# Last second products of the first pass placed between the next pass's first products, on four PSUM banks, with memory given back in two lots

## The chip, the cores and the metric

One Trainium2 chip, one core. The metric is device time in microseconds (us): how long one execution of the whole program takes. A measurement of this kernel is the median of several executions.

## What is computed

Three layers follow one another: a retention layer (attention with decay, 4 sequences of 576 tokens, 8 heads of 64), a mixture of experts in which each token goes to its best expert, and a second mixture in which every token goes through all eight experts and is weighted by a normalised gate P. The change lies in the third:

```python
def _moe2_ref(x, w_gate, w1, w2):            # x [2304,512], w1 [8,512,1024], w2 [8,1024,512]
    ...                                      # P [2304,8]: gate, normalised by rows and columns 8 times
    out = np.zeros((N, D), dtype=np.float32)
    for e in range(E):
        h = np.maximum(x @ w1[e], 0.0)
        ye = h @ w2[e]
        out += P[:, e:e + 1] * ye
    return out
```

## The kernel before

Every fp32 matrix product is made from three products of rounded parts: each operand is split into a high part (a cast, on ACT) and a low part (a subtraction, mostly on DVE), and high*high, high*low and low*high are added in PSUM.

**The third layer** runs in three passes of 768 tokens, each over the eight experts, each expert in four units (256 of the 1024 hidden columns each). In a unit the first product, x by w1, is made by a scheme with seven products of half-size blocks in place of eight. `product` 0 to 6 each issue six matmuls of 384 columns. Products 0, 2, 3 and 4 add into one PSUM bank ("x", bank 0), products 1, 5 and 6 into another ("y", bank 1). What a bank holds is read out between the products: after product 0 into the tile kp, after 2 into ku, after 3 into kv (ACT, line 1391); after product 1 DVE adds kp to the y bank (line 1397) and ACT takes the relu (line 1400); after 4 ACT takes the relu straight from the x bank (line 1403); after 5 and 6 DVE adds kv and ku. So product 2 has to wait until kp is copied, 3 until ku is, 4 until kv is, and 6 until DVE has read the y bank after 5.

**Pass 0** is written out by hand. `unit` (line 1153) puts the second products of the unit before (`second`, line 1089: three matmuls of 512 columns for one tile of 128 tokens) between its own products. They add into banks 2 to 7, one for each of the six tiles of tokens; `finish` (line 1106) weights a finished bank on DVE into an accumulator tile `a` and, at the last expert, sends it to the output with a scatter from the POOL queue. After the last unit of pass 0, its twelve calls of `second` (lines 1286 to 1290) run by themselves. Split weights come from a ring of four slots (ring_p: high and low parts, 16 KB a partition and slot), and each unit stores its split first weights in DRAM (w1s, line 1158) for passes 1 and 2.

**Passes 1 and 2** are planned: lines 1299 to 1742 make a list of tasks (engine, planned time, what they come after, which buffer they take and use), fix the order of TensorE in `line` (1611 to 1624), and play the plan through with an event loop (1656 to 1742) that gives every engine, at each moment, the startable task with the earliest due time. The order found is the order of the instructions; on the chip only semaphores hold. Buffers: five for first weights (wa, 512 KB, loaded by SP at line 1367; a unit takes four of them, one for products 0 and 1, one for 2 and 3, one for 4, one for 5 and 6), 14 for hidden values (hq), three for split hidden values (sh, sl), four for split second weights (wbh, wbl), 12 for raw second weights. The second product of an expert also has seven block products j, each as chunks (lines 1566 to 1568) for two halves of the hidden rows and three tiles of tokens. It lies one expert behind: between the first products of expert s, TensorE is given the 42 chunks of expert s-1 (GAPS says how many follow each product). For the first expert of pass 1 there is nothing to put there.

**Memory at the seam.** `with ExitStack() as m2` holds the accumulators a, `early` holds the ring and the working tiles HH, HL, p1, u2, u3 and c of pass 0. Both are given back after the last `second` (line 1292), and the tiles of passes 1 and 2 (lines 1309 to 1320: wa, wb, hq, sq, kp, ku, kv and nine accumulators ya) are laid over that memory. A new tile waits for the last readers of what lay there.

The program's names in the rows: L1100 to L1102 are the matmuls of `second`, L1385 to L1387 those of a planned product, L1566 to L1568 those of a planned chunk, L1512 a cast of a split, L219 its subtraction, L104 a scatter.

Of the kernel before, what the change touches and what calls it, by code (L numbers as in the profile page):

```python
# [28 lines left out]
RAW = 5  # L29
# [6 lines left out]
def kernel(  # L36
# [32 lines left out]
    raw_p = ctx.enter_context(tc.tile_pool(name="raw", bufs=RAW))  # L69

    early = ExitStack()
    ring_p = early.enter_context(tc.tile_pool(name="ring", bufs=4))
    sum_p = ctx.enter_context(tc.tile_pool(name="sums", bufs=1, side="right"))

# [131 lines left out]
    def load_more():  # L206
        while n_load[0] < n_known[0]:
            n = n_load[0]
            if n >= RAW and raws[n - RAW][3] * 4 > n_split[0]:
                return  # L210
            key, make, _, _ = raws[n]
            ap = make(*key)
            t = raws[n][2] = raw_p.tile([128, 1024], F32, tag="raw", name="raw")
# [7 lines left out]
    def split_step(n=1, force=False):  # L221
        for _ in range(n):
# [11 lines left out]
            if s == 0:  # L234
                c.hi = ring_p.tile([128, 2048], F32R, tag="hi", name="hi")
                c.lo = ring_p.tile([128, 2048], F32R, tag="lo", name="lo")
# [11 lines left out]
            else:  # L248
# [3 lines left out]
                if s == 0:  # L252
                    c.sums = sum_p.tile([128, 8, 128], F32, tag="sums", name="sums")
                    z = c.sums
# [31 lines left out]
    work = early.enter_context(tc.tile_pool(name="work", bufs=1))  # L286
# [10 lines left out]
    with ExitStack() as at:  # L297
# [203 lines left out]
        scr = sum_p.tile([128, 1024], F32, tag="sums", name="scr")  # L501
# [583 lines left out]
    with ExitStack() as m2:  # L1085
        sink = sinkhorn()
        ACC = {}

        def second(u, rows_, half_f, tiles_, last):

            (hh, hl), w, y = u["h"][rows_], u["w2"], u["y"]
            f0 = (2 * half_f + u["i"] % 2) * 512
            for t in tiles_:
                tick(0.648)
                s = slice((t % HT) * 128, (t % HT + 1) * 128)
                first = u["i"] == 0 and not last
                if first:
                    y[t] = bank(2 + t)
                end = u["i"] == 3 and last
                nc.tensor.matmul(y[t], hh[:, s], w.hi[:, f0:f0 + 512], start=first, stop=False)  # L1100
                nc.tensor.matmul(y[t], hh[:, s], w.lo[:, f0:f0 + 512], start=False, stop=False)  # L1101
                nc.tensor.matmul(y[t], hl[:, s], w.hi[:, f0:f0 + 512], start=False, stop=end)  # L1102
                if end:
                    finish(u["p"], u["e"], t, y[t])

        def finish(p, e, t, y):
            if e == 0:
                ACC[t] = acc_p.tile([128, DM], F32, tag=f"a{t}", name="a")
            a = ACC[t]
            sc = P[:, p * TP + t, e:e + 1]  # L1110
            if p == 0 and e == 0:
                nc.scalar.copy(a, y)
                return
            assert not gate_queue
            if e == 0:
                nc.vector.tensor_scalar(a, y, sc, None, ALU.mult)
            else:
                nc.vector.scalar_tensor_tensor(a, y, sc, a, ALU.mult, ALU.add)
            if e == E - 1:
                scatter("out", out, idc[:, p * TP + t:p * TP + t + 1], a[:])  # L1120

        def weigh():

            for t in range(TP):
                if t in WEIGH_ACT:
                    nc.scalar.activation(ACC[t], ACC[t], AF.Copy, scale=P[:, t, 0:1])
                else:
                    nc.gpsimd.tensor_scalar(ACC[t], ACC[t], P[:, t, 0:1], None, ALU.mult)

        def h_tiles(q_):  # L1130
            return HH[:, q_, :], HL[:, q_, :]

        def h_sum(u, q_, ps, add):

            c = temp("c", (128, GRP))
            nc.vector.tensor_tensor(c, ps, add, ALU.add)
            hh, hl = u["h"][q_] = h_tiles(q_)
            nc.scalar.activation(hh, c, AF.Relu)
            nc.vector.scalar_tensor_tensor(hl, c, 0.0, hh.bitcast(F32), ALU.max, ALU.subtract)

        def h_psum(u, q_, ps):
            hh, hl = u["h"][q_] = h_tiles(q_)
            nc.scalar.activation(hh, ps, AF.Relu)
            nc.vector.scalar_tensor_tensor(hl, ps, 0.0, hh.bitcast(F32), ALU.max, ALU.subtract)

        def keep(ps, tag):
            c = temp(tag, (128, GRP))
            nc.scalar.copy(c, ps)
            return c

        A = tuple(range(HT))
        Bt = tuple(range(HT, TP))
        def unit(u, pre, mids):


            w = take()
            for k, x in enumerate((w.hi, w.lo)):
                nc.sync.dma_start(out=w1s[4 * u["e"] + u["i"]][:, k], in_=x[:, 0:1792].bitcast(F32))
            arrives(5.2)
            if u["i"] % 2:  # L1160
                pre["w2"] = u["w2"] = take()
            whi = w.hi.rearrange("p (j f) -> p j f", f=128)
            wlo = w.lo.rearrange("p (j f) -> p j f", f=128)

            def product(j, ps, first):
                xh, xl = XC[j]
                tick(0.978)
                for r in range(2):
                    a, b = whi[:, 2 * j + r, :], wlo[:, 2 * j + r, :]
                    nc.tensor.matmul(ps, a, xh[:, r, :], start=first and r == 0, stop=False, skip_group_check=True)  # L1170
                    nc.tensor.matmul(ps, a, xl[:, r, :], start=False, stop=False, skip_group_check=True)  # L1171
                    nc.tensor.matmul(ps, b, xh[:, r, :], start=False, stop=r == 1, skip_group_check=True)  # L1172

            def renew(j):

                if u["last"]:
                    xsplit(j)

            def mid(k, free):
                f = mids.get(k)  # L1180
                if f:
                    f(free)
                if free is not None:
                    split_step()

            xb = bank(0, (128, GRP))
            product(0, xb, True)
            p1 = keep(xb, "p1")
            renew(0)
            mid("p0", None)  # L1190
            if pre:
                second(pre, 0, 0, A, False)
                mid("a", 1)
            yb = bank(1, (128, GRP))
            product(1, yb, True)
            h_sum(u, 0, yb, p1)
            renew(1)
            split_step()
            mid("p1", None)
            product(2, xb, False)  # L1200
            u2 = keep(xb, "u2")
            renew(2)
            mid("p2", None)
            if pre:
# [625 lines left out]
```

## Time and profile before

| | us |
|---|---|
| median of 3 runs | 1876.0 |
| the three runs | 1871.96, 1876.0, 1885.41 |
| the profiled execution | 1880.59 |
| its span, first to last instruction | 1878.8 |
| TensorE busy in it | 1803.9 (96%) |
| VectorE busy | 1233.2 (66%) |
| ScalarE busy | 892.2 (47%) |
| mean granted clock of TensorE | 0.986 |

TensorE is PE, its weight loads PEld, VectorE DVE, ScalarE ACT, GpSimd POOL, and SP the engine from whose queue most DMAs are issued. The granted clock is a share of 2.4 GHz: 1.00 is that, 0.50 is 1.2 GHz. Pass 0 of the third layer ends near 891 us, and passes 1 and 2 fill the rest.

### The profile page before, as it was taken

The page shows a single profiled execution, that of the slowest core. Times are in us where ns is not written, and L with a number is a line of the kernel's source. Part 1 is how long each engine was busy: PE and PEld are TensorE (multiplying, and loading weights), DVE is VectorE, ACT ScalarE, POOL GpSimd, SP SyncE. Part 2 cuts the span into 40 slices and gives each one's busy share as a digit, 9 for nine tenths or more (in the row PEclk, how much of TensorE's full clock was granted, in tenths as well). Part 3 has the DMA queues.
Part 4 walks back from the last instruction along what each step waited for, and adds up shares of the span by engine and source line. Part 5 has one row for each costly group of instructions (what it writes and reads, how often), then busy time and mean ns, then how long its engine had stood idle before and what let it go on. Part 6 is the DMA issues. An engine that isn't in the chain of part 4 may idle for free.

```text
span 1878.8 us, 32676 instructions
## 1 busy us (share of the span) xinstructions
PE 1803.9 (96%) x12227; PEld 1720.0 (92%) x12227; DVE 1233.2 (66%) x2239; ACT 892.2 (47%) x1718; POOL 575.1 (31%) x599
## 2 busy tenths in 40 slices
PE   7778999999999999999699999999999999999997
PEld 6657999998899999998599999999999999999997
DVE  6864446556655554555267777877887777777777
ACT  2243455544434343433355555555656555555553
POOL 4544567632332333334211121111223121111211
PEclk9998999999999999999899999999999999999998
DMA  9955555565555555543755555655556545555430
GB/s 261 239 162 176 174 196 185 175 217 184 185 186 185 185 185 204 199 174 121 229 167 152 165 160 169 186 162 153 162 165 197 155 154 161 167 158 166 145 123 35
DMA packets 194577, 325.13 MB, mean 173 GB/s; under 512 B 24547, under 2 KB 97507, under 8 KB 194408
## 3 DMA queue, kind: packets, MB, share of 16 engines
q1 hardware_dynamic: 190264, 312.29, 52.2%
q0 software_dynamic: 3712, 9.96, 1.7%
q8 instruction: 99, 1.62, 0.4%
q10 hardware_dynamic: 432, 0.69, 0.1%
q14 instruction: 70, 0.57, 0.1%
HBM read 248.28 MB, written 74.61 MB: 172 GB/s over the span
## 4 chain that ended last, share of the span: by engine, by line
PE 84%; DVE 3%; ACT 1%; issue 1%; DMA 1%; POOL 0%; SPq 0%; ACTq 0%; DVEq 0%; POOLq 0%
PE b L1568 8%; PE b L1567 8%; PE b L1566 8%; PE b L1385 8%; PE b L1386 8%; PE b L1387 8%; PE b L1100 5%; PE b L1102 5%; PE b L1101 5%; PE b L1170 4%; PE b L1172 4%; PE b L1171 4%; PE b L669 3%; PE b L671 3%; PE b L670 3%
## 5 line engine op out<-in xcount | busy, mean ns | idle before, releaser
L1566 PE MATMUL b<-wbh,sh 128*128 128x256 f32 x1344 | 379.7, 282 | 2.1 <-DVE ya L1585 2.1
L1568 PE MATMUL b<-wbh,sl 128*128 128x256 f32 x1344 | 380.3, 283 | 0.5 <-DVE sl L219 0.4
L1567 PE MATMUL b<-wbl,sh 128*128 128x256 f32 x1344 | 380.6, 283 | 0.0
L1385 PE MATMUL b<-ch,wa 128*128 128x384 f32 x896 | 304.8, 340 | 17.6 <-ACT kp L1391 7.4
L1386 PE MATMUL b<-cl,wa 128*128 128x384 f32 x896 | 302.3, 337 | 0.0
L1387 PE MATMUL b<-ch,wa 128*128 128x384 f32 x896 | 300.8, 336 | 0.0
L219 DVE TENSOR_TENSOR sl<-hq,sh 128x768 fp32r<-128x768 f32 x224 | 223.7, 1004 | 85.3 <-ACT sh L1512 83.2
L1568 PEld LDWEIGHTS b<-wbh,sl 128*128 128x128 f32 x1344 | 257.5, 192 | 0.9 <-DVE sl L219 0.9
L1566 PEld LDWEIGHTS b<-wbh,sh 128*128 128x128 f32 x1344 | 255.6, 190 | 2.3 <-ACT sh L1512 2.3
L1567 PEld LDWEIGHTS b<-wbl,sh 128*128 128x128 f32 x1344 | 257.2, 191 | 0.0
L219 POOL TENSOR_TENSOR lo<-raw,hi 128x256 fp32r<-128x256 f32 x192 | 171.8, 905 | 266.1 <-ACT hi L243 263.7
L1512 ACT CAST sh<-hq 128x768 fp32r<-128x768 f32 x224 | 184.5, 832 | 72.0 <-PE b L1567 67.3
L219 DVE TENSOR_TENSOR lo<-raw,hi 128x256 fp32r<-128x256 f32 (+1 forms) x256 | 152.2, 598 | 89.0 <-ACT hi L243 78.6
L1400 ACT ACTIVATE hq<-hq 128x384 f32<-128x384 f32 x192 | 100.9, 525 | 230.4 <-DVE hq L1397 228.4
L1385 PEld LDWEIGHTS b<-ch,wa 128*128 128x128 f32 x896 | 170.6, 190 | 22.7 <-ACT kp L1391 7.8
L1585 DVE SCALAR_TENSOR_TENSOR ya<-b,P,ya 128x256 f32<-128x256 f32 x312 | 142.2, 478 | 66.3 <-PE b L1568 65.0
L1502 POOL TENSOR_TENSOR raw<-raw 128x512 f32<-128x512 f32 x63 | 88.7, 1409 | 313.9 <-DVE wbl L219 219.6
L1386 PEld LDWEIGHTS b<-cl,wa 128*128 128x128 f32 x896 | 171.3, 191 | 0.0
L1387 PEld LDWEIGHTS b<-ch,wa 128*128 128x128 f32 x896 | 168.9, 189 | 0.0
L1170 PE MATMUL b<-ch,hi 128*128 128x384 f32 x448 | 151.6, 338 | 0.3
L1172 PE MATMUL b<-ch,lo 128*128 128x384 f32 x448 | 150.5, 336 | 0.0
L1171 PE MATMUL b<-cl,hi 128*128 128x384 f32 x448 | 150.3, 336 | 0.0
(212 smaller groups left out, 3729.8 us busy)
## 6 DMA issues: line engine op xcount, KB each, us to landing
wa<-w1s SPq DMA_DIRECT2D x192, 512.0 KB
raw<-in_moe_w_dram SPq DMA_DIRECT2D x128, 512.0 KB
w1s<-hi SPq DMA_DIRECT2D x32, 896.0 KB
w1s<-lo SPq DMA_DIRECT2D x32, 896.0 KB
raw<-in_moe_w_dram SPq DMA_DIRECT2D x108, 256.0 KB
wa<-w1s SPq DMA_DIRECT2D x64, 256.0 KB
sums<-in_moe_w_dram SPq DMA_DIRECT2D x20, 256.0 KB
kT<-in_kT_dram SPq DMA_DIRECT2D x18, 256.0 KB
```

Source lines behind the costliest of these rows:

```text
L219: eng.tensor_tensor(lo, x, hi.bitcast(F32), ALU.subtract)
L1170: nc.tensor.matmul(ps, a, xh[:, r, :], start=first and r == 0, stop=False, skip_group_check=True)
L1171: nc.tensor.matmul(ps, a, xl[:, r, :], start=False, stop=False, skip_group_check=True)
L1172: nc.tensor.matmul(ps, b, xh[:, r, :], start=False, stop=r == 1, skip_group_check=True)
L1385: nc.tensor.matmul(ps, a, xh[:, r, :], start=first, stop=False, skip_group_check=True)
L1386: nc.tensor.matmul(ps, a, xl_[:, r, :], start=False, stop=False, skip_group_check=True)
L1387: nc.tensor.matmul(ps, b, xh[:, r, :], start=False, stop=r == 1, skip_group_check=True)
L1512: nc.scalar.copy(o.tile[0], src.tile)
L1566: nc.tensor.matmul(ps, hh[:, r, c], wh[:, r], start=st, stop=False, skip_group_check=True)
L1567: nc.tensor.matmul(ps, hh[:, r, c], wl[:, r], start=False, stop=False, skip_group_check=True)
L1568: nc.tensor.matmul(ps, hl[:, r, c], wh[:, r], start=False, stop=kh == 1 and r == 1, skip_group_check=True)
L1585: nc.vector.scalar_tensor_tensor(o, ps, sc_, o, ALU.mult, ALU.add)
```

## The change

The twelve last calls of `second` become tasks of the plan (`tail`), and `line` begins with an order of its own for the first expert of pass 1: its first unit with the twelve between its products, then units 1 to 3, where a unit's products 4 and 6 stand behind product 0 of the next and product 5 goes ahead of 3. In these three units the x bank alternates between 2 and 0, product 1 stays in bank 1, and products 5 and 6 use bank 3. The memory of ring slots 0 to 2 is given back before the tail (for wa, nine hq, kp, ku, kv), that of slot 3 and the working tiles once the tail is over (for sq, wb, four more hq and three ya). The accumulators a of pass 0 are kept, and passes 1 and 2 use them with the three ya. So there are 13 hq in place of 14. The raw tiles, the sums tile and the ring become fixed tiles in place of pools that rotate. The seven second block products run in the order 0, 1, 2, 5, 3, 4, 6 for all experts, and two planned times change (POOL 1.45 to 1.3, a chunk 0.714 to 0.722).

```diff
-    early = ExitStack()
-    ring_p = early.enter_context(tc.tile_pool(name="ring", bufs=4))
+    early, late = ExitStack(), ExitStack()
+    late_p = late.enter_context(tc.tile_pool(name="late", bufs=1))
+    ringt = [None] * 3 + [late_p.tile([128, 4096], F32R, name="ring3")]
+    work = late.enter_context(tc.tile_pool(name="work", bufs=1))
+    ring_p = early.enter_context(tc.tile_pool(name="ring", bufs=1))
+    ringt[:3] = [ring_p.tile([128, 4096], F32R, name=f"ring{i}") for i in range(3)]
...
-                acc_p = m2.enter_context(tc.tile_pool(name="acc", bufs=1))
+            acc_p = ctx.enter_context(tc.tile_pool(name="acc", bufs=1, side="right"))
...
-        for ts in (A, Bt):
-            for t in ts:
-                second(u, 0 if t in A else 1, 0, (t,), False)
-                second(u, 2 if t in A else 3, 1, (t,), True)
-        release()
...
+    early.close()
+    new = fresh("early", side="right")
     free = {
-            "h": slots_of("hq", 14, (128, 2, GRP)),
+        "w1": [two(x) for x in new("wa", 5, 1024, F32R)],
+        "h": [two(x) for x in new("hq", 9, 768)],
...
+        "s": [], "w2": [],
...
-        acc = slots_of("ya", 3 * HB, (128, DM))
+    acc = [ACC[t] for t in range(2 * HB)]
+    def last_unit_done():
+        late.close()
+        new = fresh("late")
+        free["s"] += ...
+        free["w2"] += ...
+        free["h"] += [two(x) for x in new("hr", 4, 768)]
+        acc.extend(new("ya", HB, 512))
...
+    JORD = (0, 1, 2, 5, 3, 4, 6)
...
+    tail = []
+    for ts in (A, Bt):
+        for t in ts:
+            for n, (q, half_f) in enumerate(((0, 0), (2, 1)) if t in A else ((1, 0), (3, 1))):
+                tail.append(Task("PE", 0.69, lambda _, q=q, half_f=half_f, t=t, n=n: second(pre, q, half_f, (t,), n == 1), tail[-1:]))
...
+            where = {"x": 2 * (i % 2) if s == E else 0, "y": 1, "y5": 3 if s == E and i else 1}
...
+        if s == E:
+            early_banks = [tail[-1], relu[2, 2], relu[2, 3], a0, a1]
+            u, rest, line0 = line0, list(tail), []
+            for n, j in zip((1, 2, 2, 2, 2, 2, 1), range(7)):
+                line0 += [u[0][j], *rest[:n]]
+                rest = rest[n:]
+            line0 += rest
+            line0 += [u[1][j] for j in (0, 1, 2, 5, 3)]
+            for i in range(1, 4):
+                if i < 3:
+                    line0.append(u[i + 1][0])
+                line0 += [u[i][4], u[i][6]]
+                if i < 3:
+                    line0 += [u[i + 1][j] for j in (1, 2, 5, 3)]
...
-            accs = {t: acc[t + (2 * HB if p == 2 and t < HB else 0)] for t in range(2 * HB)}
+        accs = {t: t + (2 * HB if p == 1 and t < HB else 0) for t in range(2 * HB)}
...
-            for j in range(7):
+        for j in JORD:
```

## Rows read from the trace of the kernel before

**Rows 1.** The page, busy share of TensorE in 40 slices
```profile
PE   7778999999999999999699999999999999999997
```

**Rows 2.** Stages (window, busy of PE, PEld, DVE, ACT, POOL, clock, DMA share, GB/s)
```profile
890.00:900.00 10.00, 3.06 (x17) 2.59 (x15) 1.16 (x2) 0.03 (x1) 3.46 (x7) 0.79 0.89 298
900.00:910.00 10.00, 8.36 (x24) 7.08 (x24) 0.56 (x1) 2.92 (x6) 2.54 (x2) 0.53 0.67 212
910.00:940.00 30.00, 22.83 (x120) 20.23 (x120) 10.63 (x16) 13.38 (x26) 7.72 (x6) 1.00 0.68 210
950.00:1830.00 880.00, 878.36 (x6226) 877.45 (x6225) 675.49 (x1012) 482.73 (x861) 169.15 (x130) 1.00 0.53 162
```

**Rows 3.** Waits of PE between 880 and 960 us (total, times, longest)
```profile
PE b L1385 <- ACT kp L1391: 7.4, 1, 7.4
PE b L1385 <- ACT ku L1391: 3.8, 4, 2.0
PE b L1385 <- DVE hq L1397: 2.9, 4, 0.7
PE b L1385 <- ACT kv L1391: 2.3, 4, 0.6
```

**Rows 4.** Chain of waits from 880 to 960 us, and the timeline of ACT
```profile
893.15 6.72 DMA out_dram<-a,idc
...
899.97 0.48 ACT L1391 COPY kp<-b 128x384 f32<-128x384 f32 x1 [15.23 <-DMA out_dram<-a,idc]
```

**Rows 5.** Timeline of PE (start, duration, line; in brackets idle before and releaser)
```profile
882.63 0.39 PE L1100 MATMUL b<-hi,HH 128*128 128x512 f32 x1
...
890.82 0.34 PE L1385 MATMUL b<-ch,wa 128*128 128x384 f32 x1
...
904.16 0.52 PE L1387 MATMUL b<-ch,wa 128*128 128x384 f32 x1
904.48 0.52 PE L1385 MATMUL b<-ch,wa 128*128 128x384 f32 x1
...
917.21 0.44 PE L1385 MATMUL b<-ch,wa 128*128 128x384 f32 x1 [2.00 <-ACT ku L1391]
...
919.09 0.45 PE L1385 MATMUL b<-ch,wa 128*128 128x384 f32 x1 [0.57 <-ACT kv L1391]
...
943.37 0.34 PE L1385 MATMUL b<-ch,wa 128*128 128x384 f32 x1
...
945.13 0.34 PE L1385 MATMUL b<-ch,wa 128*128 128x384 f32 x1
...
946.17 0.28 PE L1566 MATMUL b<-wbh,sh 128*128 128x256 f32 x1
```

**Rows 6.** Timeline of ACT ahead of the wait at 917 us
```profile
915.42 0.83 ACT L1512 CAST sh<-hq 128x768 fp32r<-128x768 f32 x1
916.16 0.61 ACT L1512 CAST wbh<-raw 128x512 fp32r<-128x512 f32 x1
```

**Rows 7.** SP: its timeline, stages of its two loads, and a wait
```profile
866.32 1.30 SPq L1367 DMA_DIRECT2D wa<-w1s  x2
...
870.00:871.00 1.00, 1.00 (x7) 0.96 (x6) 0.00 (x0) 0.00 (x0) 1.00 (x1) 1.00 1.01 391
871.00:872.00 1.00, 1.00 (x8) 1.00 (x7) 0.47 (x1) 0.00 (x0) 0.92 (x2) 1.00 0.08 29
...
SPq L1367 <- PE b L1102: 33.8, 2, 23.3
```

**Rows 8.** Timeline of DVE and PE near the end of pass 2
```profile
1845.49 0.94 DVE L219 TENSOR_TENSOR sl<-hq,sh 128x768 fp32r<-128x768 f32 x1
...
1844.93 0.55 PE L1566 MATMUL b<-wbh,sh 128*128 128x256 f32 x1 [2.10 <-DVE ya L1585]
1845.28 0.42 PE L1567 MATMUL b<-wbl,sh 128*128 128x256 f32 x1
1845.49 0.42 PE L1568 MATMUL b<-wbh,sl 128*128 128x256 f32 x1
```

More of the change, by code (lines that the diff above doesn't have):

```diff
@@ new lines, with second @@
+    sink = sinkhorn()
+    ACC = {}
+    def second(u, rows_, half_f, tiles_, last):
+        (hh, hl), w, y = u["h"][rows_], u["w2"], u["y"]
+        f0 = (2 * half_f + u["i"] % 2) * 512
+        for t in tiles_:
+            tick(0.648)
+            s = slice((t % HT) * 128, (t % HT + 1) * 128)
+            first = u["i"] == 0 and not last
+            if first:
+                y[t] = bank(2 + t)
+            end = u["i"] == 3 and last
+            nc.tensor.matmul(y[t], hh[:, s], w.hi[:, f0:f0 + 512], start=first, stop=False)
+            nc.tensor.matmul(y[t], hh[:, s], w.lo[:, f0:f0 + 512], start=False, stop=False)
+            nc.tensor.matmul(y[t], hl[:, s], w.hi[:, f0:f0 + 512], start=False, stop=end)
+            if end:
+                finish(u["p"], u["e"], t, y[t])
@@ new lines, in finish @@
+    def finish(p, e, t, y):
+        if e == 0:
+            ACC[t] = acc_p.tile([128, DM], F32, name=f"a{t}")
+        a = ACC[t]
+        sc = P[:, p * TP + t, e:e + 1]
+        if p == 0 and e == 0:
+            nc.scalar.copy(a, y)
+            return
+        assert not gate_queue
+        if e == 0:
+            nc.vector.tensor_scalar(a, y, sc, None, ALU.mult)
+        else:
+            nc.vector.scalar_tensor_tensor(a, y, sc, a, ALU.mult, ALU.add)
+        if e == E - 1:
+            scatter("out", out, idc[:, p * TP + t:p * TP + t + 1], a[:])
@@ new lines, with cut, fresh @@
+    HB = GRP // 128
+    two = lambda a: a.rearrange("p (k f) -> p k f", k=2)
+    f32 = lambda a: a.bitcast(F32)
+    def cut(a, sizes):
+        o, r = 0, []
+        for n in sizes:
+            r.append(a[:, o:o + n])
+            o += n
+        return r
+    def fresh(name, **more):
+        q = ctx.enter_context(tc.tile_pool(name=name, bufs=1, reuse_waits="tile", **more))
+        return lambda name, n, size, dt=F32: [q.tile([128, size], dt, name=f"{name}{i}") for i in range(n)]
+    early.close()
@@ new lines @@
+    line += b
+    clock_ = 0.0
+    for t in line:
+        t.ideal = clock_
+        clock_ += t.us
+    for t in tasks:
+        for a in t.after:
+            a.next.append(t)
+    order, left = [], {t: len(t.after) for t in tasks}
+    ready = [t for t in tasks if not left[t]]
+    while ready:
+        t = ready.pop()
+        order.append(t)
+        for n in t.next:
+            left[n] -= 1
+            if not left[n]:
+                ready.append(n)
+    assert len(order) == len(tasks)
```

1074 lines of the change are left out of this document (511 added, 563 removed).

## Prediction

> **What bounds the kernel now.** I read the page's 40 slices first, to see where TensorE is not full. From the fifth slice to the last but one it shows nine tenths or more everywhere but in the twentieth, 893 to 940 us, which has six [rows 1]. So the kernel is bound by TensorE, and outside that slice only its start and its end have room. The stages then give the size of the hole: 3.1 us of work from 890 to 900, a clock of 0.53 from 900 to 910 (near the lower level, 1.2 GHz), and idle parts with the clock back at 1.00 from 910 to 940; from 950 to 1830 TensorE is idle for 1.6 us of 880 [rows 2]. The waits name the causes: one of 7.4 us for the copy into kp, and 12 smaller ones for ku, kv and the y bank, 9.0 us together [rows 3]. The chain says what kp waited for: not its product but the scatter of pass 0's accumulators, 6.72 us of DMA; ACT sat for 15.23 us until it was done [rows 4]. kp is laid over an accumulator's memory, and must not be written until the scatter has read it.
>
> **The seam before, in numbers.** The twelve calls of `second` run from 882.63 to 890.82, 8.19 us. The 28 first products of the first expert follow from 890.82 to 943.37, where the next expert's first product starts. One undisturbed product takes 946.17 - 945.13 = 1.04 us [rows 5], 28 take 29.12. The work is 8.19 + 29.12 = 37.31 us, the stretch is 943.37 - 882.63 = 60.74, the loss 23.43. Of it 16.4 us are the waits [rows 3]. At the lower clock matmuls start 904.48 - 904.16 = 0.32 us apart [rows 5] in place of 1.04/6 = 0.173; some 27 of them between 900.5 and 909.3 cost 27 x 0.147 = 4.0. The last 3.0 are the slower first matmuls after 13 waits.
>
> **The change, part by part.**
>
> *The accumulators stay.* kp no longer lies where the scatter reads, so the 7.4 us go. What is late next: product 0 of the first unit has ended, one call of `second` (0.68), product 1 (1.04) and two more calls (1.36) lie between it and product 2, 3.1 us against a copy that takes 0.48 [rows 4]. TensorE then has no long gap before 900 us, and the 4.0 us at the lower clock go with it.
>
> *The twelve calls between the products of unit 0.* Where a product waits for a copy or for DVE, it now has two calls, 1.36 us, ahead of it. The uncovered chain is the start-to-start time across a wait less one product: 919.09 - 917.21 - 1.04 = 0.84 us [rows 5], refill included. It is hidden. The DVE work of `finish` and the scatters are the same as before, and lie beside TensorE.
>
> *Units 1 to 3 on four banks.* By the new order one product, 1.04 us, stands between the one whose bank is copied and the one that needs the copy; the chain of 0.84 fits with 0.2 to spare. Product 6 has two ahead of it. One place stays open: in unit 3 product 4 follows product 3 directly, 0.84 us. That cover of 0.2 is thin. ACT works in its order, and a cast that stands ahead of a copy delays it: at 917 us two casts of 0.83 and 0.61 us made a wait, otherwise of 0.57, one of 2.00 [rows 5, 6]. That happened once in four units. The new units have the same seven or so casts (three sh, four wbh, as many as there are buffers) in 22 us in place of 35, with all of them startable at once when the tail is over. Below, no such hit: 0. Above, one for each of the seven casts less the cover, 7 x 0.5 = 3.5, and as much for DVE's subtractions ahead of its additions: 7. I take 1.5, one hit like that at 917, as the row nearest to it.
>
> *Memory in two lots.* Before, SP issued two loads of wa at 866 us; the next had to wait 23.3 us for the last `second` [rows 7], and the loads of raw weights stood behind it in SP's queue. The new wa lies over ring slots that pass 0 is done with, or over memory free since its start, so unit 0 has its weights early, and DMA has less to do at the seam. In units 2 and 3 a load has to turn round faster: each tile's last product is some five products, 5.2 us, before the product that needs the next load. The two loads issued together at 866.32 had landed by about 871.1, 4.8 us later for both [rows 7]. Below 0; above, six loads of these two units each held up by one more of 512 KB, at 391 GB/s 1.3 us: 8. I take 0, because one load alone takes less than two. sq and wb wait for the last call of `second`, but are not needed before the 38th us.
>
> *13 hq in place of 14; other order of j; planned times.* In the steady part TensorE waits for next to nothing [rows 2], so the order cannot gain there. One buffer fewer can only cost: 0 below, and above 15 experts (all of the two passes but the first) x two halves x one subtraction of 0.94 us [rows 8], on which the buffer's release would hang: 28 us. I take 0: in between lie product 0 and several chunks of TensorE work. At the end of pass 2 TensorE waits 2.10 us for a DVE read of its bank, and then runs some 14 matmuls 1845.49 - 1845.28 = 0.21 us apart, at the lower clock, where at the upper one they would take half [rows 8]: 2.1 + 14 x 0.1 = 3.5. The new order has the same first three block products, so the same wait can stay, go or double: -3.5 to +3.5, I take 0.
>
> *The fixed raw, ring and sums tiles* wait for the same readers as the rotating ones: 0, between -1 and +1 us, the waits of the steady part.
>
> **The sum.** New stretch: 37.31 + 0.84 + 1.5 = 39.65 us, against 60.74: 21.1 us less. The profiled execution took 1880.6 (span 1878.8); it becomes 1859.5, a factor of 0.9888. It is 4.6 us above the median of 1876.0, and the factor puts the median at 1855.0.
>
> **A rule that speaks against it.** With waits of 0.6 to 0.7 us several times in each 10 us, the clock between 910 and 940 us was 1.00 throughout [rows 2, 3]; it fell only with the single 7.4 us wait. The Trainium skill ("TensorE: Matmul & The Clock Gate", section "A second HAM failure mode: psum-queue depth-cycling") says that a kernel which cycles through PSUM banks can idle so briefly and so often that its clock swings between the two levels. By that rule units 1 to 3 would run at the lower level; the trace does not agree for the pattern before, and the new one has fewer such gaps.
>
> **The rivals.**
> - *Weights or queues take over in units 1 to 3.* For it: three units use 1.8 MB each in 7.3 us, some 250 GB/s, when the stretch before moved 210 to 298 [rows 2]. Against: 391 GB/s in row 870 [rows 7], and SP is free earlier. Price: 5 to 10 us more, about 1862.
> - *The clock falls in units 1 to 3*, as a mechanism here: small waits at each bank turn, 21 products at 6 x 0.32 = 1.92 in place of 1.04: 18.5 us, giving 1873.5. Against it: the clock of 1.00 among 12 such waits.
> - *The buffer that is missing costs each expert* (the other side). In each later expert the fourth hidden write waits until a split has let a buffer go, its addition stands at the head of DVE's queue, and product 1 of the next unit waits for that bank. Two waits of 0.94 us in 15 experts make 28 us: 1855 + 28 = 1883. It is slower than before from 21.1/15 = 1.4 us an expert. For it: DVE is 77% busy (675.49 of 880). Against: TensorE's 1.6 idle us in that stretch leave no sign that the buffers were short.
> - *It doesn't do what it says*: kp or a weight still waits for the scatters. 7.4 + 4.0 come back: 1866.
> - *The end improves too*: 3.5 less, 1851.5.
>
> **How the numbers follow.** The forecast has 0.72; its own bounds are 1850 to 1861 (no hit, 1.5 us less, or up to 3 us more of hits, and some 3 us by which medians of such runs move, since the three shown lie 4 below to 9 above theirs). Weights 0.12, clock 0.04, missing buffer 0.05, not as said 0.02, end 0.05. The range reaches from 1849 to 1866: it takes in the forecast, the weights and the end. A change of 1% of 1876, 18.8 us, is about what a measurement of this kernel can tell from none; it lies at 1857.2, close to the forecast. I give the forecast's case 0.73 to be below that, so 0.72 x 0.73 + 0.05 = 0.58 for faster. Slower by over 1% needs 40 us beyond the forecast, 0.02 of the missing buffer's 0.05. The rest, 0.40, is within 1%.
>
> **What would show it.** Right: no wait for kp; the calls of `second` and first products mixed; a clock of 1.00 from 880 to 930; the first chunk of the second product near 923 us (944.4 before); waits of PE in the seam of 1 to 4 us in sum; from there to the end the same length. Wrong: many waits for ku and kv of more than 0.5 us, or matmuls that wait for DMA into wa (weights); 0.32 us distances in units 1 to 3 (clock); waits of products for DVE hq spread over 950 to 1830 (buffer); an ACT copy into kp that waits for out_dram (not as said).

## The result, and the profile after

The changed kernel took 1853.0 us in the median (1850.1 to 1858.1) where the kernel before took 1876.1 (1872.0 to 1885.4): a ratio of 0.987, with a 95% interval of 0.983 to 0.992. The forecast was 1855.0. A second measurement, on another occasion (e11 below), gave 1862.1 against 1881.4, a ratio of 0.991 (0.988 to 0.994). So the change is worth 0.9 to 1.3%.

The page of the changed kernel: busy share of TensorE in 40 slices, and the clock granted in them.

```profile
PE   7878999999999999999999999999999999999997
...
PEclk9999999999999999999999999999999999999999
```

The six of the twentieth slice [rows 1] is a nine. The stages around the seam (window, busy of PE, PEld, DVE, ACT, POOL, clock, DMA share, GB/s), and the long stretch behind it:

```profile
870.00:880.00 10.00, 10.00 (x53) 9.16 (x52) 5.67 (x8) 5.01 (x9) 5.08 (x4) 1.00 0.42 136
880.00:890.00 10.00, 9.38 (x47) 8.09 (x46) 3.47 (x5) 1.45 (x4) 4.53 (x9) 1.00 1.02 374
890.00:900.00 10.00, 9.10 (x51) 8.31 (x50) 7.25 (x9) 6.26 (x13) 8.41 (x7) 1.00 0.69 215
900.00:910.00 10.00, 10.00 (x57) 9.66 (x56) 2.70 (x5) 3.98 (x10) 3.88 (x3) 1.00 0.90 303
910.00:920.00 10.00, 9.43 (x59) 9.07 (x59) 4.57 (x7) 5.22 (x11) 0.00 (x0) 1.00 0.75 242
950.00:1830.00 880.00, 876.93 (x6231) 875.94 (x6230) 675.71 (x1023) 480.70 (x851) 172.17 (x131) 1.00 0.51 156
```

Where 3.06 of 10 us were worked from 890 to 900, and a clock of 0.53 was granted from 900 to 910 [rows 2], TensorE now works nine tenths and more at 1.00. The waits of PE from 865 to 955 us (total, times, longest) are three lines in place of the four of [rows 3], 2.1 us in place of 16.4, and none for kp:

```profile
PE b L1455 <- DVE hq L1467: 0.9, 2, 0.6
PE b L1455 <- ACT p L1461: 0.6, 1, 0.6
PE b L1455 <- ACT u L1461: 0.6, 1, 0.6
```

The timeline of PE has the borders of the seam and every wait in it (lines 1455 to 1457 are now those of a planned product, 1602 to 1604 those of a chunk, 1103 to 1105 those of `second`):

```profile
874.17 0.34 PE L1455 MATMUL b<-ch,wa 128*128 128x384 f32 x1
...
888.87 0.44 PE L1455 MATMUL b<-ch,wa 128*128 128x384 f32 x1 [0.62 <-DVE hq L1467]
...
890.71 0.34 PE L1455 MATMUL b<-ch,wa 128*128 128x384 f32 x1
...
892.18 0.45 PE L1455 MATMUL b<-ch,wa 128*128 128x384 f32 x1 [0.27 <-DVE hq L1467]
...
894.15 0.45 PE L1455 MATMUL b<-ch,wa 128*128 128x384 f32 x1 [0.63 <-ACT p L1461]
...
912.99 0.44 PE L1455 MATMUL b<-ch,wa 128*128 128x384 f32 x1 [0.57 <-ACT u L1461]
...
915.17 0.34 PE L1455 MATMUL b<-ch,wa 128*128 128x384 f32 x1
...
916.21 0.28 PE L1602 MATMUL b<-wb,sq 128*128 128x256 f32 x1
```

Measured as in the prediction, from the first of the seam's matmuls to the next expert's first product, the seam takes 915.17 - 874.17 = 41.00 us in place of 60.74 [rows 5]. Its work is 37.31 us as before, so the loss is 3.69 in place of 23.43. The first wait is that of product 6 of unit 0, which stands between the last two calls of `second`. Unit 1 begins at 890.71, and the next two waits are those of its products 1 and 2. The timelines of DVE and ACT show why:

```profile
887.60 0.75 DVE L1121 SCALAR_TENSOR_TENSOR a<-b,P,a 128x512 f32<-128x512 f32 x1 [1.69 <-PE b L1105]
888.27 0.55 DVE L1467 TENSOR_TENSOR hq<-b,u 128x384 f32<-128x384 f32 x1
...
892.59 1.12 ACT L1548 CAST wb<-raw 128x512 fp32r<-128x512 f32 x2
893.62 0.47 ACT L1461 COPY p<-b 128x384 f32<-128x384 f32 x1
```

The addition of line 1467, on which the product at 888.87 waits, stands behind the weighting of a bank of `second` (line 1121), and that weighting waits for a call of `second` that TensorE works after the addition's own product. It stands ahead because it is issued with the call. The wait at 892.18 is for the next such addition. Five microseconds after the first wait a copy stands behind two casts of split weights, and the product at 894.15 waits for that copy. The fourth wait, at 912.99, in unit 3, is the place that the prediction called open.

Three lengths account for the profiled executions (span 1850.1 against 1878.8, 28.7 us less): ahead of the seam 8.5 us less, in the seam 19.7, and behind it 0.5 (from the next expert's first product to the end 934.93 in place of 935.43). Nothing shows the 8.5 to be work of the change, for equal programs scatter by as much there. In the 14 profiled executions of this study the seam starts between 869.8 and 883.8 us: twice for the changed kernel itself, at 874.17 and 869.78, and twice for one variant of the kernel before (e3 and e9), at 872.30 and 880.44.

### The profile page after: what moved, and what is told of

Its sections match the earlier page's. It is cut to its first block, busy times and chain, and to the rows that moved or that the text cites. A ratio compares the mean times of both kernels' runs of the same rounds, so it can differ in the third digit from the quotient of the medians.

```text
span 1850.1 us, 32843 instructions
## 1 busy us (share of the span) xinstructions
PE 1796.5 (97%) x12227; PEld 1716.1 (93%) x12227; DVE 1227.7 (66%) x2239; ACT 892.4 (48%) x1718; POOL 577.0 (31%) x599
## 4 chain that ended last, share of the span: by engine, by line
PE 85%; DVE 4%; issue 1%; ACT 1%; POOL 0%; ACTq 0%; POOLq 0%; DVEq 0%
PE b L1455 8%; PE b L1603 8%; PE b L1604 8%; PE b L1602 8%; PE b L1456 8%; PE b L1457 8%; PE b L1105 5%; PE b L1103 5%; PE b L1104 5%; PE b L1173 4%; PE b L1175 4%; PE b L1174 4%; PE b L673 3%; PE b L675 3%; PE b L674 3%
## 5 line engine op out<-in xcount | busy, mean ns | idle before, releaser
L1604 PE MATMUL b<-wb,sq 128*128 128x256 f32 x1344 | 378.0, 281 | 1.1 <-DVE sq L226 1.1
L1602 PE MATMUL b<-wb,sq 128*128 128x256 f32 x1344 | 377.4, 281 | 1.0 <-DVE a L1625 1.0
L1603 PE MATMUL b<-wb,sq 128*128 128x256 f32 x1344 | 378.2, 281 | 0.0
L1604 PEld LDWEIGHTS b<-wb,sq 128*128 128x128 f32 x1344 | 254.1, 189 | 1.5 <-DVE sq L226 1.5
L1602 PEld LDWEIGHTS b<-wb,sq 128*128 128x128 f32 x1344 | 253.9, 189 | 1.3 <-ACT wb L1548 1.2
L1603 PEld LDWEIGHTS b<-wb,sq 128*128 128x128 f32 x1344 | 254.2, 189 | 0.0
L226 POOL TENSOR_TENSOR ring<-raw,ring 128x256 fp32r<-128x256 f32 x192 | 170.8, 901 | 265.3 <-ACT ring L249 213.7
L226 DVE TENSOR_TENSOR ring<-raw,ring 128x256 fp32r<-128x256 f32 (+1 forms) x256 | 157.9, 620 | 84.5 <-ACT ring L249 75.1
L226 DVE TENSOR_TENSOR sq<-hq,sq 128x768 fp32r<-128x768 f32 x167 | 166.8, 1003 | 68.8 <-ACT sq L1548 68.6
L1455 PE MATMUL b<-ch,wa 128*128 128x384 f32 x448 | 152.0, 339 | 2.1 <-DVE hq L1467 0.9
L1455 PE MATMUL b<-c,wa 128*128 128x384 f32 x448 | 151.6, 338 | 1.0 <-ACT u L1461 1.0
L1173 PE MATMUL b<-ch,ring 128*128 128x384 f32 x448 | 151.6, 338 | 0.3
L1456 PE MATMUL b<-c,wa 128*128 128x384 f32 x448 | 151.3, 338 | 0.0
L1456 PE MATMUL b<-cl,wa 128*128 128x384 f32 x448 | 151.3, 338 | 0.0
L1457 PE MATMUL b<-c,wa 128*128 128x384 f32 x448 | 150.9, 337 | 0.0
L1457 PE MATMUL b<-ch,wa 128*128 128x384 f32 x448 | 150.8, 337 | 0.0
L1175 PE MATMUL b<-ch,ring 128*128 128x384 f32 x448 | 150.5, 336 | 0.0
L1174 PE MATMUL b<-cl,ring 128*128 128x384 f32 x448 | 150.3, 336 | 0.0
```

What stands on the lines that cost most here:

```text
L226: eng.tensor_tensor(lo, x, hi.bitcast(F32), ALU.subtract)
L1455: nc.tensor.matmul(ps, a, xh[:, r, :], start=first, stop=False, skip_group_check=True)
L1456: nc.tensor.matmul(ps, a, xl_[:, r, :], start=False, stop=False, skip_group_check=True)
L1602: nc.tensor.matmul(ps, hh[:, r, c], wh[:, r], start=st, stop=False, skip_group_check=True)
L1603: nc.tensor.matmul(ps, hh[:, r, c], wl[:, r], start=False, stop=False, skip_group_check=True)
L1604: nc.tensor.matmul(ps, hl[:, r, c], wh[:, r], start=False, stop=kh == 1 and r == 1, skip_group_check=True)
```

## The experiments

Each seam below is measured in the same way. The kernels of e1, e2, e5, e6, e7, e8 and e12 start from the changed kernel, those of e3, e4, e9 and e10 from the kernel before; e11 is the changed kernel itself.

| run | seam us | seam to end us | median us | ratio to before (95%) |
|---|---|---|---|---|
| before | 60.74 | 935.43 | 1876.1 | |
| changed | 41.00 | 934.93 | 1853.0 | 0.987 (0.983 to 0.992) |
| e1, no mixing, no rotation | 49.66 | 935.20 | 1865.6 | 0.994 (0.992 to 0.996) |
| e2, no rotation | 48.16 | 936.13 | 1862.3 | 0.992 (0.988 to 0.995) |
| e3, kept warm | 60.23 | 936.07 | 1873.9 | 0.998 (0.997 to 1.000) |
| e4, fixed tiles alone | 59.85 | 935.37 | 1877.9 | 1.000 (0.998 to 1.003) |
| e5, j in plain order | 42.07 | 937.33 | 1857.6 | 0.991 (0.988 to 0.995) |
| e6, 14 hq | 41.47 | 937.33 | 1858.1 | 0.990 (0.987 to 0.993) |
| e7, weighting planned | 40.77 | 935.19 | 1855.3 | 0.989 (0.986 to 0.992) |
| e8, and the gap filled | 39.85 | 937.38 | 1851.0 | 0.987 (0.984 to 0.990) |
| e9, e3 again | 61.65 | 935.81 | 1879.7 (one run) | |
| e10, kept warm twice | 57.32 | 934.28 | 1871.8 | 0.995 (0.993 to 0.997) |
| e11, changed again | 41.52 | 937.30 | 1862.1 | 0.991 (0.988 to 0.994) |
| e12, POOL and DVE apart | 39.85 | 935.58 | 1857.3 | 0.988 (0.985 to 0.990) |

In e8 and e12 the next expert's first product lies inside the seam, so theirs is taken to the product that now stands directly ahead of the first chunk. Up to the chunk itself e8 takes 40.89 us and the changed kernel 42.04 (916.21 - 874.17). In the runs of e9 to e12 the kernel before took 1881.4 us, 5 more than in the others: absolute times of different rows are not comparable to better than that, seams are.

### e1 and e2: the three parts, one after the other

```diff
 # e1: the memory as changed, the order of the kernel before
-            where = {"x": 2 * (i % 2) if s == E else 0, "y": 1, "y5": 3 if s == E and i else 1}
+            where = {"x": 0, "y": 1, "y5": 1}
...
-            for n, j in zip((1, 2, 2, 2, 2, 2, 1), range(7)):
-                line0 += [u[0][j], *rest[:n]]
-                rest = rest[n:]
...
+            line0 += rest + u[0]
+            line0 += [u[i][j] for i in range(1, 4) for j in range(7)]
 # e2: unit 0 mixed as in the change, units 1 to 3 as in e1
```

> The changed kernel with its memory, but the twelve calls of second by themselves ahead of the first products, and these in the old order on banks 0 and 1. My theory: the wait of kp for the scatters (7.4 us) and the time at the lower clock behind it (4.0) go by the memory alone, the 12 small waits of the four units (9.0) and their slow first matmuls (3.0) stay. Seam, from the first call of second to the first product of the next expert: 37.3 + 12.0 = 49.3 us (60.7 before, 41.0 changed); time some 1864.5. Rival, the order does it and the memory alone only trades the wait for kp for another wait (weights, a tile of the second lot): seam above 55 us, time above 1870.

> The changed kernel with the twelve calls between the products of unit 0, but units 1 to 3 in the old order on banks 0 and 1. My theory: the three waits of each of these units come back, 3 units x 3 x 0.84 us = 7.6 more than hidden; unit 0 stays covered. Seam 41.0 + 7.6 - 0.8 (the one open place of the new order is among the nine) = 47.8 us; waits of TensorE for ku and kv about 0.6 each, for the y bank 0.7. Rival, the rotation is worth little because the queues of ACT and DVE set the pace of these units: seam below 44 us.

Both came out as the theory had it: 49.66 and 48.16 us. The waits of PE in the seam of e1 (total, times, longest):

```profile
PE b L1455 <- ACT u L1461: 5.1, 8, 0.9
PE b L1455 <- DVE hq L1467: 3.9, 4, 1.7
```

and in that of e2:

```profile
PE b L1455 <- ACT u L1461: 3.6, 6, 0.6
PE b L1455 <- DVE hq L1467: 3.0, 5, 0.7
PE b L1455 <- ACT p L1461: 0.6, 1, 0.6
```

In neither does TensorE wait for the copy p of unit 0, which was kp before (the 0.6 of e2 is unit 1's), and in both the granted clock was 1.00 in each 10 us from 870 to 940. So the new memory, the kept accumulators and the two lots together, is worth 60.74 - 49.66 = 11.1 us without the new order, mixing unit 0 another 1.5, and the new order of units 1 to 3 on four banks 48.16 - 41.00 = 7.2. Accumulators kept with the memory given back in one lot were not run. In e1 the small waits of units 1 to 3 are all still there, as in [rows 3]. What the memory takes away is the one long wait and the low clock behind it.

### e4: the fixed tiles

```diff
-            t = raws[n][2] = raw_p.tile([128, 1024], F32, tag="raw", name="raw")
+            t = raws[n][2] = rawt[n % RAW]
...
-                c.hi = ring_p.tile([128, 2048], F32R, tag="hi", name="hi")
-                c.lo = ring_p.tile([128, 2048], F32R, tag="lo", name="lo")
+                c.hi, c.lo = (ringt[j % RING][:, 2048 * n:2048 * (n + 1)] for n in range(2))
```

> The kernel before with only its raw tiles, sums tile and ring made fixed tiles, as in the change. In the profile of the changed kernel the seam starts 8.5 us earlier than in that of the kernel before. My theory: that is scatter of the part before 300 us, and the fixed tiles change nothing: time within 4 us of before, and the start of the seam somewhere between 874 and 885 us. Rival, the fixed tiles shorten the part before the seam: seam starts near 874 us, time 1868.

As the theory had it: a ratio of 1.000 (0.998 to 1.003), a seam that starts at 881.08 us, and takes 59.85 with a wait for kp of 5.9 in place of 7.4.

### e3, e9 and e10: the clock by itself

The prediction priced the low clock at 4.0 us and held that it came with the 7.4 us wait alone. To see it by itself, throw-away matmuls were put into that wait:

```diff
+            if t is line[1]:
+                p7 = bank(2, (128, GRP))
+                for _ in range(36):
+                    nc.tensor.matmul(p7, XC[0][0][:, 0, 0:128], XC[0][0][:, 0, :], start=True, stop=True)
```

> The kernel before, with 36 matmuls of 384 columns into a bank that is free, put behind the first two products of the seam, so that TensorE works while kp waits for the scatters; their result is not used. My theory: the wait itself stays (kp is copied at the same distance from the last scatter, and product 2 starts as late), but the clock stays at 1.00, and the 4.0 us between 900 and 909 us go: seam 56.7 us in place of 60.7, time 1872. Rival, the copies between the products hide the lower clock: seam 60 us or more.

The clock did hold through the filled wait, of which 1.3 us were left, but the seam took 60.23 us. The stages of e3:

```profile
895.00:900.00 5.00, 4.28 (x25) 3.96 (x24) 2.34 (x4) 2.92 (x7) 1.88 (x2) 1.00 0.53 163
900.00:905.00 5.00, 3.00 (x14) 2.69 (x13) 3.12 (x4) 2.87 (x6) 1.27 (x1) 0.85 0.86 269
905.00:910.00 5.00, 4.43 (x14) 3.92 (x14) 0.00 (x0) 0.97 (x2) 2.46 (x2) 0.50 0.46 145
```

and its timeline of PE where the clock falls:

```profile
901.27 0.34 PE L1387 MATMUL b<-ch,wa 128*128 128x384 f32 x1
903.61 0.69 PE L1385 MATMUL b<-ch,wa 128*128 128x384 f32 x1 [2.00 <-ACT ku L1391]
```

The fall had only moved, behind the 2.00 us wait for ku. In the kernel before the same wait, at 917.21 [rows 5], did not lower it. Two runs were made to tell chance from cause: the same kernel once more, and one with 10 more such matmuls in the place of the 2.00 us wait.

```diff
-            if t is line[1]:
+            if t in (line[1], line[9]):
                 p7 = bank(2, (128, GRP))
-                for _ in range(36):
+                for _ in range(36 if t is line[1] else 10):
```

> The kernel of e3 once more. Theory (the clock falls after the 2.00 us wait because of that wait, which stands in the order of this kernel): again 1.00 in the stretch of the 36 extra matmuls, again about 0.5 for some 5 us behind the wait for ku, and a seam near 60.2 us. Rival (the fall in e3 was chance): no fall, and a seam of 56.7 us.

> The kernel of e3 with 10 more throw-away matmuls (1.7 us) in the place of the 2.00 us wait for ku, so that some 0.3 us of it are left. Theory (what the lower clock takes in this seam is 3.5 to 4 us, and it is there only because TensorE stands still for two microseconds or more): the clock is 1.00 from 870 to 940, the seam is 60.2 less 3.5 = 56.7 us, and the median is 1876.8 less 4.0 = 1872.8 us. Rival (the clock falls behind another wait in its turn): a seam of 59 us or more.

e9 did it again. Its stages:

```profile
905.00:910.00 5.00, 4.43 (x24) 4.11 (x24) 3.22 (x6) 2.92 (x6) 1.30 (x1) 1.00 0.54 159
...
913.00:918.00 5.00, 4.43 (x14) 3.83 (x13) 0.00 (x1) 0.97 (x2) 2.67 (x3) 0.50 0.60 187
```

and its timeline of PE (the clock is down from the second wait on: 0.69 us for a matmul in place of 0.45):

```profile
911.95 0.45 PE L1385 MATMUL b<-ch,wa 128*128 128x384 f32 x1 [2.00 <-ACT ku L1391]
...
914.21 0.69 PE L1385 MATMUL b<-ch,wa 128*128 128x384 f32 x1 [0.57 <-ACT kv L1391]
```

In e10 the clock is 1.00 in every 10 us from 870 to 940, the 2.00 us wait is 0.24, and the seam is 57.32 us: 0.6 over the theory and 1.7 below the rival. The copy into kp released TensorE 17.85 us after the start of the seam in e10 and 17.87 in the kernel before, so the two seams differ by the clock alone, as far as the trace shows: it costs 60.74 - 57.32 = 3.4 us here. Filling the first wait alone did not bring them back, filling both did. The median fell by more than that (0.995 means 9 us, 5 at the near end of the interval). Some 1.2 us of that fall lie behind the seam, where the stretch to the end took 934.28 us in place of 935.43. Where the others lie was not traced.

### e5 and e6: the order of j, and the buffer that is missing

```diff
 # e5
-    JORD = (0, 1, 2, 5, 3, 4, 6)
+    JORD = (0, 1, 2, 3, 4, 5, 6)
 # e6
-        free["h"] += [two(x) for x in new("hr", 4, 768)]
+        free["h"] += [two(x) for x in new("hr", 5, 768)]
```

> The changed kernel with the second block products in the old order 0 to 6. My theory: TensorE waits for next to nothing between the seam and the end with either order, so the stretch from the next expert's first product to the end of the span stays at 934.9 us within 1.5, and the time at 1853. Rival, the new order is worth the shorter wait at the end (1.02 us in place of 2.10, without the time at the lower clock behind it): the stretch becomes 937 us or more, with a wait of 2 us for the DVE read of a bank near the end.

> The changed kernel with 14 buffers for hidden values in place of 13. My theory: the missing one costs nothing; the stretch from the next expert's first product to the end stays at 934.9 us within 1.5, the waits of TensorE between 950 and 1800 us (2.1 us in sum with 13) stay about 2. Rival, the missing buffer costs each expert: the stretch gets shorter by more than 2 us and the waits fall below 1.

With 14 buffers the waits between 950 and 1800 us are not smaller (2.3 us in sum, 2.1 with 13), so the missing buffer costs nothing that shows. The 934.9 us of both theories was missed: the stretch behind the seam took 937.33 us in both, 2.4 more than in the changed kernel, with a wait of 2.1 us for DVE near the end in place of 1.0. For e5 alone that reads as a gain of the new order, as the rival has it. But e6 keeps the new order and shows the same, so the order is not its cause (e11 shows what differs). Each of the two also had a wait in the seam that the changed kernel's first profile does not have. In e5:

```profile
903.97 0.44 PE L1455 MATMUL b<-ch,wa 128*128 128x384 f32 x1 [0.93 <-DMA wa<-w1s]
```

and in e6:

```profile
907.84 0.44 PE L1455 MATMUL b<-ch,wa 128*128 128x384 f32 x1 [0.36 <-DMA wa<-w1s]
```

The changed kernel itself had 0.4 us of it in e11. In all three it is the first product of unit 3. Its load of weights is close to late: TensorE waited up to 0.9 us for it in three of the seven profiles with the full new order, and not at all in the other four.

One more loss lies behind the seam, and no wait shows it. The matmul 6000 places behind the next expert's first one, in the kernel before and in the changed kernel:

```profile
1791.43 0.28 PE L1566 MATMUL b<-wbh,sh 128*128 128x256 f32 x1
...
1764.99 0.28 PE L1602 MATMUL b<-wb,sq 128*128 128x256 f32 x1
```

Counted from the end of the seam it starts after 1791.43 - 943.37 = 848.06 us and 1764.99 - 915.17 = 849.82. The waits up to there add to 1.2 and 1.4 us, so 1.6 of the 1.8 us between them are no waits. In e3, e4, e9 and e10 the same matmul starts after 847.9 to 848.6 us, in e1, e2, e5, e6, e7 and e11 after 849.6 to 849.8. The distance grows evenly, by some 0.1 us an expert: the matmuls of a planned product start 0.175 us apart in place of 0.174, those of a chunk 0.119 in both. So it is neither the order of j, the number of hq, the new order of the seam nor the fixed tiles. The kernels that have it share the new places of the tiles in memory and the planned times; which of these it is was not tried.

### e7 and e8: the four waits that are left

In e7 the weighting of a finished bank is a DVE task of the plan, with its own due time, and not issued with the call of `second`. e8 adds to it that the next expert's first product goes into the open place of unit 3.

```diff
 # e7
-                tail.append(Task("PE", 0.69, lambda _, ...: second(pre, q, half_f, (t,), n == 1), tail[-1:]))
+                tail.append(Task("PE", 0.69, lambda _, ...: second(pre, q, half_f, (t,), n == 1, False), tail[-1:]))
+            done_.append(Task("DVE", 0.66, lambda _, t=t: finish(pre["p"], pre["e"], t, pre["y"][t]), tail[-1:]))
 # e8, on top
+    line.remove(g1[E + 1, 0, 0])
+    line.insert(line.index(g1[E, 3, 4]), g1[E + 1, 0, 0])
```

> The changed kernel with the weighting of a finished bank (finish) as a task of its own on DVE after its last call of second, in place of being put into DVE's queue together with that call. My theory: the three waits at 888.9, 892.2 and 894.2 us (0.62, 0.27, 0.63) have one cause, that a weighting which is not ready stands ahead of an addition that is; the relu and two casts on ACT then come late too. All three go: seam 41.0 - 1.5 - 0.5 (slow first matmuls) = 39.0 us. Rival, the third wait comes from the casts alone, which become startable when the tail is over: it stays, seam 39.8 us.

> As e7_finish_task, and the next expert's product 0 is put between products 3 and 4 of unit 3, the one place where nothing stands between a bank that is copied and the product that needs the copy. My theory: the wait of 0.57 us there goes with its slow first matmul; from the start of the seam to the first chunk it takes 42.0 - 2.0 - 0.8 = 39.2 us (42.0 changed), and the time is some 2.8 us below the changed kernel, 1850. Rival, the wait only moves to the products behind it: 40 us or more.

The cause was right: the first three waits are gone from e7, and the one of unit 3 from e8. The gain was not. e7 has a seam of 40.77 us where its theory had 39.0, and e8 takes 40.89 up to the first chunk in place of 39.2, the time that its rival had. In e7 two waits, of unit 1's products 3 and 6, came in the place of three:

```profile
898.32 0.44 PE L1456 MATMUL b<-ch,wa 128*128 128x384 f32 x1 [0.56 <-ACT u L1462]
...
902.69 0.45 PE L1456 MATMUL b<-ch,wa 128*128 128x384 f32 x1 [0.99 <-DVE hq L1468]
```

Both are in e8 too, at 897.83 and 902.21. The timelines of DVE and POOL of e8 show what the addition of the second stood behind:

```profile
899.65 2.04 DVE L226 TENSOR_TENSOR sq<-hq,sq 128x768 fp32r<-128x768 f32 x1
901.61 0.55 DVE L1468 TENSOR_TENSOR hq<-b,u 128x384 f32<-128x384 f32 x1
...
899.26 4.93 POOL L1360 TENSOR_TENSOR raw<-raw,raw 128x512 f32<-128x512 f32 x3 [0.69 <-POOL raw L1363]
```

A subtraction that takes 0.94 to 0.96 us elsewhere took 2.04, while POOL worked on its own subtractions. The first wait goes back to the same: its copy stood behind a relu whose addition, at 896.80 in e7, came late behind two such subtractions beside one of POOL's:

```profile
894.48 2.40 DVE L226 TENSOR_TENSOR wb<-raw,wb 128x512 fp32r<-128x512 f32 x2 [0.21 <-ACT wb L1549]
...
894.48 1.85 POOL L1360 TENSOR_TENSOR raw<-raw,raw 128x512 f32<-128x512 f32 x1
```

e8 took 1851.0 us (1846.0 to 1859.7) where the changed kernel had taken 1853.0: the two can't be told apart.

### e11 and e12: the wait near the end

In the changed kernel and in e1 and e7 the wait for DVE near the end was 1.0 us; before, and in e2 to e6 and e8 to e10, it was 2.1. The last two runs ask what decides it. e11 is the changed kernel again. e12 is e8 with POOL's last subtraction given to DVE:

```diff
-            t4 = Task("POOL", 1.3, sub(B[1, 0], B[1, 0], B[0, 0]), ...)
+            t4 = Task(*(("DVE", 0.6) if s == n_exp - 1 and kh else ("POOL", 1.3)), sub(B[1, 0], B[1, 0], B[0, 0]), ...)
```

> The changed kernel once more, with nothing edited. Theory (the 1.0 or 2.1 us wait of the second product near the end belongs to the order of a kernel's instructions): 1.0 us again, POOL's last subtraction about 3.8 us long and VectorE's beside it 0.94, from the next expert's first product to the end 934.9 us; no wait for wa in the seam; seam 41 us; 1853 us. Rival (which of the two engines is held up is settled anew in each execution): the wait may be 2.1 us, POOL's subtraction 1.5, VectorE's 2.05 and the rest 937.3 us.

> The kernel of e8 with POOL's last subtraction for the last expert (1.5 us beside VectorE's 2.05 us one in e8) given to VectorE, as 0.6 us of work in its own queue. Theory (the 2.05 us subtraction is long because POOL's runs beside it): all of VectorE's subtractions of 128x768 take 0.94 to 0.96 us, the wait of the second product for VectorE near the end is 1.0 to 1.6 us in place of 2.1, the granted clock there is 1.00, the rest is 935 to 936 us in place of 937.4, and the median is 1851.0 less 1.5 = 1849.5 us. Rival (the long one has another cause): a subtraction of 2.05 us and the 2.1 us wait stay, and the rest is 937.4 us or, with 0.6 us more on VectorE, 938.

The timelines of POOL, DVE and PE near the end, of the changed kernel's first profile:

```profile
1814.52 3.83 POOL L1360 TENSOR_TENSOR raw<-raw,sums 128x512 f32<-128x512 f32 x1 [5.42 <-DVE wb L226]
...
1813.92 0.94 DVE L1360 TENSOR_TENSOR hq<-hq,hq 128x768 f32<-128x768 f32 x1
1814.79 0.94 DVE L226 TENSOR_TENSOR sq<-hq,sq 128x768 fp32r<-128x768 f32 x1
...
1817.75 0.36 PE L1602 MATMUL b<-wb,sq 128*128 128x256 f32 x1 [1.02 <-DVE a L1625]
```

and of e11, the same kernel:

```profile
1810.62 1.50 POOL L1360 TENSOR_TENSOR raw<-raw,sums 128x512 f32<-128x512 f32 x1 [5.42 <-DVE wb L226]
...
1810.01 0.95 DVE L1360 TENSOR_TENSOR hq<-hq,hq 128x768 f32<-128x768 f32 x1
1810.88 2.05 DVE L226 TENSOR_TENSOR sq<-hq,sq 128x768 fp32r<-128x768 f32 x1
...
1814.94 0.35 PE L1602 MATMUL b<-wb,sq 128*128 128x256 f32 x1 [2.11 <-DVE a L1625]
```

The theory of e11 fell, and its rival holds: with nothing edited, the wait is 1.0 in one execution and 2.1 in another. The two subtractions start 0.27 and 0.26 us apart, and one engine holds the other up: POOL's takes 3.83 us and DVE's 0.94, or POOL's 1.50 and DVE's 2.05. With the 2.11 us wait the clock then fell to 0.66 from 1815 to 1820, and the rest was 937.30 us. In e12 there is nothing to meet there:

```profile
1823.23 0.94 DVE L226 TENSOR_TENSOR sq<-hq,sq 128x768 fp32r<-128x768 f32 x1
...
1826.19 0.36 PE L1603 MATMUL b<-wb,sq 128*128 128x256 f32 x1 [1.01 <-DVE a L1626]
```

The wait is 1.0 and the rest 935.58, as the theory had it, though one execution can't show that it always is. Its time, 1857.3 us (1853.2 to 1861.4), stands beside 1862.1 (1850.4 to 1871.6) for the changed kernel in the same runs. The theory's 1849.5 did not come, and the ratio to the kernel before, 0.988, is no better than the 0.987 of e8: no gain shows in the time.

## Why the prediction was right

The time, the sign and the cause came out as forecast: 1853.0 us for 1855.0, and 21.1 us at the seam of which 19.7 were measured. That the time came within 2 us of the forecast is in part luck: the second measurement gave 1862.1 (e11), and equal programs reach the seam 4 to 8 us apart.

- **The accumulators stay, 7.4 + 4.0 us.** Right: 11.1 us with the new memory and without the new order (e1). The 4.0 by itself measured 3.4 (e10). It counted some 27 matmuls at the lower clock between 900.5 and 909.3 us; 22 start there in the trace, of 24 from 900 to 910 [rows 2]. That the low clock hung on the 7.4 us wait alone was too simple. Filling that wait alone left the clock loss in place (e3, e9). It was gone in e1, where the longest wait left was 1.7 us.
- **The twelve calls hidden between the products of unit 0.** This step failed in part. It took the DVE work of `finish` to lie beside TensorE, since its amount is unchanged. Its place in DVE's queue is not: it is issued with the call of `second`, and so stands ahead of the additions that the next products wait for. Three waits of 1.5 us in sum came of it, one in unit 0 and two at the start of unit 1: 0.9 behind that queue, and 0.6 behind two casts on ACT, which the same queue had made late, for all three went when the weighting got its own place (e7). Mixing unit 0 gained 1.5 us net (e1 to e2).
- **Units 1 to 3 on four banks, 0.84 + 1.5 us.** The open place cost its wait of 0.57 us and a slow first matmul, as worked out. For a cast that hits a copy it took 1.5 us. There was one such hit, on unit 1's product 2, with a wait of 0.63, and the two waits ahead of it were behind DVE's queue. Start to start, with the slow matmuls behind them, the three took 2.37 us in place of 1.5. With 0.84 for the open place, and 0.48 spread over products that took 1.05 to 1.17 us, that is the loss of 3.69 against the 2.34 of the sum. The four banks took 7.2 us away (e2).
- **Memory in two lots, 0.** Right within a microsecond. The load for the first product of unit 3 is waited for in some executions, 0.4 to 0.9 us, so the rival of late weights was the right place to look, at a tenth of its price.
- **13 hq, 0.** Right (e6). The busy share of DVE, for which the rival spoke, was not the limit there.
- **Other order of j, between -3.5 and +3.5, taken as 0.** The swing was there, 2.4 us of the 3.5, and its source was not the order: in the changed kernel it is settled in each execution by which of POOL and DVE is held up (e11). With the 2.1 us wait and the low clock behind it, the stretch behind the seam is 937.3 or 937.4 in e5, e6, e8 and e11, against 935.4 to 936.1 in the kernel before, e3, e4 and e9; with the 1.0 us wait it is 934.9 to 935.6. So one to two microseconds of the change are given back there, evenly over the experts and not in waits. Neither e5 nor e6 took that away, so order and buffer are not it, and the cause stays open between the places of the tiles and the planned times.
- **The fixed tiles, 0.** Right (e4).
- **The rule that spoke against it.** In units 1 to 3 the clock was 1.00, and so it was in e1 and e2 among 12 waits each of 0.3 to 1.7 us. The rival that the clock falls there is out. The Trainium skill ("TensorE: Matmul & The Clock Gate", section "A second HAM failure mode: psum-queue depth-cycling") has a kernel swing between the levels on brief idle times as it cycles through PSUM banks. The traces do not agree for the short waits here. The one fall in each of e3 and e9 came with a wait of 2.00 us, and no run shows whether it is what that section means.

## What to carry to other kernels

When memory given back at a seam is laid under new tiles, look at who reads it last. Here a scatter to DRAM did, and one small copy that waited for it held up TensorE for 7.4 us and lowered its clock: the new memory was over half of the gain at the seam. When matmuls of two phases are interleaved, plan the other engines' follow-up work too, since what is issued with a matmul takes a place in a queue ahead of what the next matmul waits for. And judge a change of one wait by several executions, because one trace may show a wait of 1.0 or of 2.1 us for the same program.

## What was not expected of the hardware

- **POOL and DVE hold each other up.** Subtractions with two operands in SBUF, started 0.26 us apart, took 1.50 us on POOL and 2.05 on DVE, or 3.83 and 0.94, in two executions of one program (e11). Alone they took about 1.3 and 0.94. The 2.04 us subtraction of e8 is another such meeting. The Trainium skill ("SBUF — State Buffer", section "SBUF: two separate sides") says that DVE and GpSimd lock one pair of ports for a whole instruction, and that the other waits: the sums agree, since in e11 the 1.50 us less the 0.26 leave 1.24, and 0.81 more, near the 0.87 at which such subtractions follow one another there, make the 2.05 of DVE. It also says that the one that starts first gets the pair. These traces neither confirm nor refute that: when POOL's subtraction is recorded to start, an earlier one of DVE with two SBUF operands is already under way in both (since 1813.92 and 1810.01). What they show is that behind it either engine may come next.
- **A wait of 2.0 us lowered the clock in some executions and not in others.** The one for ku did in e3 and e9, where the longer wait ahead of it had been filled and some 0.6 us waits stood between. It did not in the kernel before and in e4, where the clock had fallen before and was back at 1.00 from 910 us, for a wait that ends at 917.21 [rows 2, 5], and from 909, for one that ends at 914.46. Near the end a 2.1 us wait was followed by a fall in e11 (0.66) and by none in e2 and e10, in the same place of the work. What decides it, these runs do not show.
